# Attention with beacons and a low-rank mixer on one core: first roundings, pair order and the rounding of U and V moved

## The chip, the core and the metric

One core of a Trainium2 chip. Five engines run side by side, each through its own list of instructions in order: TensorE (matrix products and transposes, into PSUM), VectorE, ScalarE, GpSimd (named POOL in the profile) and SyncE (SP). SyncE, ScalarE and GpSimd also issue DMA transfers; only GpSimd's change the number type on the way. PSUM is used as eight tiles in rotation. The metric is the time of one execution on the device, in microseconds (us), lower is better.

## The reference

```python
def _attn_ref(q, k, v, beacon_k, beacon_v):         # 8 batches, 8 heads, 576 tokens, width 64; 16 beacons
    k_all = np.concatenate([beacon_k, k], axis=2)
    v_all = np.concatenate([beacon_v, v], axis=2)
    scores = scale * np.matmul(q, k_all.transpose(0, 1, 3, 2))
    scores = np.where(causal, -1000000000.0, scores)
    a = np.exp(scores - scores.max(-1, keepdims=True))
    a /= a.sum(-1, keepdims=True) + 1e-09
    return np.matmul(a, v_all)

def _moe_ref(x, U, V, w_ch1, w_ch2):                # x: the heads side by side, 576 x 512 per batch
    h = x.transpose(0, 2, 1) @ U @ V                # U: 576 x 32, V: 32 x 576
    u = x + h.transpose(0, 2, 1)
    ch = np.maximum(u @ w_ch1, 0.0) @ w_ch2         # 512 -> 2048 -> 512
    return u + ch
```

All tensors come and go in float32; the kernel computes in 16 bits.

## The kernel before

The work is a row of 32 pairs of heads, four per batch; pair 0 is heads 0 and 1 of batch 0. For a pair, q and k are transposed by TensorE and copied out of PSUM by VectorE (L276), for pair 0 in halves by ScalarE and VectorE. The scores of both heads go into PSUM in two visits of two column groups each (`score_units`, matmuls in L312). Before the products of a visit small matmuls (L304) put the causal mask in, from `identb` and `negmask`. ScalarE turns each group into exponentials (L318), into the tiles `expt`. The values product `av_unit` (L339) multiplies them by `vs`, v with a column of ones, five row blocks one after the other: block j needs the rows of v up to block j. VectorE divides (L347, L348).

When a batch has all eight heads, `mix_units` applies U and V (L368, L404, L416), and `mlp_units` makes units of the channel mixer: sixteen `g_unit` per 512 tokens, four matmuls each (L443), which need `w1`, and then `c_unit` (L459), which need `w2`. Units stand in a queue and are let in between the steps of attention, `FIRST[p]` of them in pair p.

The order on each engine is the order in which the program is written (`tc.manual_schedule`). The start goes so:

- `load_first`: SyncE and ScalarE load q and k of pair 0 and q of pair 1 as float32 (`stq`, `stk`). GpSimd loads the beacon keys.
- `build_masks`: GpSimd makes the identity, issues the load of pair 1's k, and makes the triangular mask; VectorE makes `identb`, `bigmask` and `negmask` from these.
- GpSimd then issues the other half of k and q of batch 0, the beacons of v and the first half of v (L201).
- VectorE fills the gaps of the four `expt` tiles with zeros, and VectorE and ScalarE round first q, then k of pair 0 to 16 bits, each one half (`regroup`, L246, in ScalarE's case L579); k's beacon rows follow (L249).
- `keep_warm` issues matmuls of 128x128 by 128x512 that nobody reads: `IDLE[0]` of them before the first transposes, `IDLE[1]` before pair 0's scores, `IDLE[2]` before pair 1's, `IDLE[3]` before later ones.
- TensorE: pair 0's transposes, its first and second visit, pair 1's transposes (q from `prs[1]`, a rounding by VectorE; k from what GpSimd loaded), pair 1's first visit.
- GpSimd issues the first half of batch 1's k and q, its beacon keys, the second half of v, and the first quarter of `w1` (`emit_w1`).

Then the loop over the eight pairs of batches 0 and 1 begins. Pair p's turn holds the transposes of pair p+2, the second visit of pair p+1, the values products of pair p, and the first visit of pair p+2. In the turn of pair 0, behind the transposes, `load_rest` is called. It begins with `small_loads`: VectorE clears one column of a float32 tile, SyncE loads U in three parts (L151 to L155) and V in four copies (L157) into it, and GpSimd rounds U (L161) and V (L162, L165) to 16 bits. Then GpSimd issues the second half of k and q of batch 1, its beacons and the first half of its v, and the rest of the weights:

```python
def load_rest():
    small_loads()()
    token_load(nc.gpsimd, k[1], kt, HALVES[1])
    token_load(nc.gpsimd, q[1], qt, HALVES[1])
    v_beacon(beacon_v[1], vss[1])
    v_tokens(v[1], vss[1], HALVES[0])
    emit_w1(1)
```

The second half of k and q of batch 1 is first read by the transposes of pair 6 (heads 4 and 5 of batch 1; L260), which open pair 4's turn.

Of the kernel before, what the change touches and what calls it, by code (L numbers as in the profile page):

```python
# [11 lines left out]
F32 = mybir.dt.float32  # L12
# [6 lines left out]
P = 128  # L19
F16_MAX = 65504.0  # L20
# [10 lines left out]
def kernel(  # L31
# [13 lines left out]
    nc = tc.nc  # L45
    B, H, S, D = q.shape
    Nb = beacon_k.shape[2]
# [22 lines left out]
    SLOT = 496  # L70
    EW = 4 * SLOT

    blk = {}
# [14 lines left out]
    gw = [max(o + w for _, _, w, o in g) for g in groups]  # L88
# [13 lines left out]
    def pst(shape, dtype, name):  # L102
        return psum.tile(shape, dtype, tag="ps", name=name)


    ident = const.tile([P, P], F16, name="ident", tag="ident")
    mask = const.tile([P, P], F16, name="mask", tag="mask")
    bigmask = const.tile([P, 4, P], F16, name="bigmask", tag="bigmask")
    identb = const.tile([P, P], BF16, name="identb", tag="identb")
    negmask = const.tile([P, 2, P], BF16, name="negmask", tag="negmask")  # L110

    def build_masks():
        make_identity(nc, ident)
        token_load(nc.gpsimd, k[0], Ls[0][0][0], SETS[1])
        make_upper_triangular(nc, mask, val=F16_MAX, diag=True)
        nc.vector.memset(bigmask[:, 0, P - Nb : P], F16_MAX)
        nc.vector.tensor_copy(out=identb, in_=ident)
        nc.vector.tensor_copy(out=bigmask[:, 0, 0 : P - Nb], in_=mask[:, Nb:P])
        nc.vector.tensor_copy(out=bigmask[:, 1, :], in_=mask)
        for i in range(2):  # L120
            nc.vector.tensor_scalar(
                out=negmask[:, i, :], in0=bigmask[:, i, :], scalar1=1.0, scalar2=NEG,
                op0=ALU.is_lt, op1=ALU.mult,
            )
        for c in range(2, 4):
            nc.vector.tensor_copy(out=bigmask[:, c, :], in_=mask)

    w1 = const.tile([P, NCC, FF], F16, name="w1", tag="w1")
    w2 = const.tile([P, NDC, DM], F16, name="w2", tag="w2")
# [11 lines left out]
    NE = 4  # L141
    expts = [const.tile([P, EW], F16, name=f"expt{i}", tag=f"expt{i}") for i in range(NE)]
# [3 lines left out]
    def small_loads():  # L146

        f = utp.tile([P, NT * R + S], F32, name="small", tag="ut")
        nc.vector.memset(f[:, 0:1], 0.0)
        uf, vf = f[:, 0 : NT * R].rearrange("p (j r) -> p j r", r=R), f[:, NT * R :]  # L150
        nc.sync.dma_start(out=uf[: nq[0], 0, :], in_=moe_U[0 : nq[0], :])  # L151
        nc.sync.dma_start(
            out=uf[:, 1 : NT - 1, :], in_=moe_U[q0[1] : QM, :].rearrange("(j p) r -> p j r", p=P)
        )
        nc.sync.dma_start(out=uf[:NL, NT - 1, :], in_=moe_U[QM:S, :])  # L155
        for cc in range(NCC):
            nc.sync.dma_start(out=vf[ds(R * cc, R), :], in_=moe_V)  # L157

        def cast():
            for rr, jj in ((nq[0], slice(0, 1)), (P, slice(1, NT - 1)), (NL, slice(NT - 1, NT))):  # L160
                nc.gpsimd.tensor_copy(out=Usb[:rr, jj, :], in_=uf[:rr, jj, :])  # L161
            nc.gpsimd.tensor_copy(out=Vsb, in_=vf[:, 0:QM])  # L162
            for cc in range(NCC):
                rs = ds(R * cc, R)
                nc.gpsimd.tensor_copy(out=Vend[rs, cc, :], in_=vf[rs, QM:S])  # L165

        return cast
# [17 lines left out]
    def token_load(eng, src, dst, hs):  # L185
        eng.dma_start(out=dst[0:TP, hs, :], in_=src[hs].rearrange("h (p j) d -> p h (j d)", j=TJ))
# [7 lines left out]
    def v_beacon(bsrc, vs):  # L194
        beacon_load(nc.gpsimd, bsrc, by_head(vs)[:, 0, :, 0:D], ALLH)

    def v_tokens(src, vs, hs, js=range(NT)):
        dst = by_head(vs)[:, :, hs, 0:D]
        for j in js:
            a = Nb if j == 0 else 0  # L200
            nc.gpsimd.dma_start(  # L201
                out=dst[a : a + nq[j], j, :, :], in_=src[hs, ds(q0[j], nq[j]), :].rearrange("h p d -> p h d")
            )
# [24 lines left out]
    def keep_warm(ps, n, a=ident):  # L228


        w = ps.shape[-1] // P
        for _ in range(n):
            nc.tensor.matmul(
                ps[:, 0 : w * P].rearrange("p (a b) -> p a b", b=P), a,
                a.rearrange("p (a b) -> p a b", a=1).broadcast_to([P, w, P]),
                start=True, stop=True,
            )

    def regroup(st, c, i, *copies, beacons=None):

        t = pairs.tile([P, TJ, 2, D], F16, name=f"pr{i}", tag=f"pr{i}")
        src = by_token(st[i][:, 2 * c : 2 * c + 2, :])
        w = TJ // len(copies)
        for a, copy in enumerate(copies):
            js = slice(w * a, w * (a + 1))
            copy(out=t[0:TP, js], in_=src[0:TP, js])  # L246
        if i == 0:
            b = beacons if beacons is not None else src
            copies[0](out=t[TP:TB, TJ - 1], in_=b[TP:TB, TJ - 1])  # L249
        return t  # L250
# [312 lines left out]
    first = []  # L563
# [15 lines left out]
        nc.scalar.activation(out=out, in_=in_, func=AF.Copy)  # L579

    prs = {}

    def regroup_of(p):
        b, c = divmod(p, NH2)
# [16 lines left out]
    def qkT_of(p):  # L601
        b, c = divmod(p, NH2)
        new_qT_of(p)
        copies = [(act_copy, nc.vector.tensor_copy) if p == 0 else (nc.vector.tensor_copy,)] * 2
        turns = by_heads(Ls[b][0], c)
        for i, t in enumerate(prs.get(p, ())):
            if t is not None:
                turns[i] = in_pair(prs[p])[i]
        return qkT_units(turns, qTs[b], kTs[b % 2], c, copies)

    def scores_of(p):
        b, c = divmod(p, NH2)
        return score_units(c, qTs[b], kTs[b % 2], [expts[(2 * p + i) % NE] for i in range(2)], p < NM)
# [19 lines left out]

    QUOTA = {2: 4}

    IDLE = [8, 0, 1, 0]
    queue = []
    state = {"t": 0}

# [38 lines left out]
    with tc.manual_schedule(engines={ENG.PE, ENG.Activation, ENG.DVE, ENG.SP, ENG.Pool}):  # L678
# [3 lines left out]
            token_load(nc.gpsimd, src, dst, HALVES[1])  # L682
        v_beacon(beacon_v[0], vss[0])
        v_tokens(v[0], vss[0], HALVES[0])
        for i in range(NE):

            nc.vector.memset(expts[i][:, SLOT + gw[1] : 2 * SLOT], 0.0)
            nc.vector.memset(expts[i][:, 3 * SLOT + gw[3] : blk[(3, 4)] + P], 0.0)
        V = nc.vector.tensor_copy
        prs[0] = [None, regroup(first, 0, 1, V, act_copy)]  # L690
        prs[0][0] = regroup(first, 0, 0, V, act_copy, beacons=by_token(Ls[0][0][0][:, 0:2, :]))
        keep_warm(pst([P, 512], F32, name="idle"), IDLE[0], plain)
        t0, sc = qkT_of(0), scores_of(0)
        for u in t0:
            u()
        sc[0](IDLE[1])
        sc[1]()
        masks = sc[2]
        prs[1] = [None, regroup(first, 1, 1, V)]
        for u in qkT_of(1):  # L700
            u()
        sc = scores_of(1)
        sc[0](IDLE[2])

# [6 lines left out]
        emit_w1(0)  # L711

        def load_rest():
            small_loads()()
            token_load(nc.gpsimd, k[1], kt, HALVES[1])
            token_load(nc.gpsimd, q[1], qt, HALVES[1])
            v_beacon(beacon_v[1], vss[1])
            v_tokens(v[1], vss[1], HALVES[0])
            emit_w1(1)
            v_tokens(v[1], vss[1], HALVES[1])  # L720
            emit_w1(2)
            emit_w1(3)
            emit_w2()

        NP1 = NF * NH2
        for p in range(NP1):
# [14 lines left out]
            sc = []  # L741
# [170 lines left out]
```

## Time and profile before

| | before |
|---|---|
| median of 3 runs | 360.89 us (360.02 to 362.49) |
| profiled execution | 359.93 us |
| its span, first to last instruction | 358.2 us |
| ScalarE's first run of exponentials starts at | 8.12 us |
| share of the span on the chain that ended last, by TensorE | 86% |

All times inside the execution are counted from the start of the span. The 1.7 us between span and time lie around it. In the rows an engine's name is followed by the line of the kernel, the operation, what is written <- what is read, the sizes, and how many such instructions in a row; the times at the front are start and length, and a bracket gives the idle time before and what ended it. The windows view gives, for each stretch, its length, the busy time of TensorE, of its weight loads, of VectorE, ScalarE and GpSimd with counts, then the mean clock that was granted to TensorE (1.00 is full), the DMA share and GB/s. A row of a DMA ends with the size and the median time from issue to landing.

### The profile page before, as it was taken

Reading aid. Unit: us, or ns where it says so; the run is one execution under the profiler, and the core shown is the slowest. Engines: PE = TensorE matmul, PEld = TensorE weight load, DVE = VectorE, ACT = ScalarE, POOL = GpSimd, SP = SyncE. Lnnn points to the kernel's source line nnn. Section 1 sums busy time; section 2 is a strip of 40 time slices with the busy share of each in tenths; the row PEclk is TensorE's granted clock in tenths of the full one; section 3 lists DMA queues with packets and bytes.
Section 4 is the critical chain, followed back from the end, with each engine's and each line's share of the span. In section 5 each row is a group of like instructions: output and inputs, shape, how many; then the busy total and the mean of one; then the engine's idle time right before and its main releaser. Section 6 shows DMA issues by size and latency. Waiting matters only on the chain.

```text
span 358.2 us, 7821 instructions
## 1 busy us (share of the span) xinstructions
PE 347.8 (97%) x3130; PEld 174.0 (49%) x3130; DVE 187.6 (52%) x485; ACT 166.2 (46%) x356; POOL 97.3 (27%) x139
## 2 busy tenths in 40 slices
PE   6998999999999999999999999999999999999995
PEld 2565455455565444444444444444454444444444
DVE  5585653578986444563456446445645522313311
ACT  4886761469645364367444654456503202401400
POOL 8749611609139028403820400000000000000000
PEclk9898999999999999999999999999999999999999
DMA  8979999999999949995999793142013414013212
GB/s 168 147 111 153 173 208 185 194 173 135 121 76 138 198 103 114 153 198 88 147 143 192 129 135 94 60 100 55 31 60 88 67 59 105 15 59 90 30 51 73
DMA packets 143946, 41.37 MB, mean 115 GB/s; under 512 B 128800, under 2 KB 139296, under 8 KB 143904
## 3 DMA queue, kind: packets, MB, share of 16 engines
q0 software_dynamic: 87408, 18.18, 65.3%
q1 hardware_dynamic: 56272, 22.34, 31.3%
q8 instruction: 26, 0.43, 0.5%
q10 hardware_dynamic: 224, 0.30, 0.3%
q14 instruction: 16, 0.13, 0.1%
HBM read 37.59 MB, written 9.44 MB: 131 GB/s over the span
## 4 chain that ended last, share of the span: by engine, by line
PE 86%; DMA 5%; DVE 3%; SPq 2%; POOL 1%; issue 1%; ACT 0%; POOLq 0%; DVEq 0%
PE gps L443 35%; PE cps L459 32%; PE po L339 7%; PE sps L312 7%; DMA uT<-xb 2%; PE tps L254 2%; DMA small<-in_moe_V_dram 2%; DMA st<-in_q_dram 1%; PE cph L484 1%; SPq L359 1%; DVE kT L276 1%; PE qtp L368 1%; DVE uT L386 1%; DVE qT L276 1%; PE ups L404 1%
## 5 line engine op out<-in xcount | busy, mean ns | idle before, releaser
L318 ACT ACTIVATE expt<-sps 128x496 f16<-128x496 f32 (+2 forms) x256 | 111.4, 534 | 63.9 <-PE sps L312 63.9
L443 PE MATMUL gps<-uT,w 128*128 128x512 f16 x576 | 136.0, 381 | 0.0
L459 PE MATMUL cps<-w,gT 128*128 128x512 f16 x560 | 132.7, 380 | 0.0
L447 ACT ACTIVATE gT<-gps 128x512 f16<-128x512 f32 x86 | 51.9, 608 | 96.3 <-PE gps L443 96.2
L443 PEld LDWEIGHTS <-w 128*128 128x128 f16 x576 | 52.2, 98 | 59.6 <-issue 3.7
L459 PEld LDWEIGHTS <-gT 128*128 128x128 f16 x560 | 49.9, 98 | 59.2 <-issue 6.8
L449 DVE TENSOR_SCALAR gT<-gps 128x512 f16<-128x512 f32 x58 | 40.0, 690 | 48.3 <-PE gps L443 47.2
L472 DVE TENSOR_TENSOR ob<-cps,ut 128x512 f32<-128x512 f32 x31 | 21.4, 690 | 49.6 <-PE cps L459 46.7
L339 PEld LDWEIGHTS <-expt 128*128 128x128 f16 (+1 forms) x960 | 37.0, 98 | 15.7 <-issue 2.5
L201 POOL DMA_DIRECT2D vs<-in_v_dram x50 | 39.6, 807 | 16.3 <-PE po L339 4.2
L339 PE MATMUL po<-vs,expt 128*128 128x65 f16 (+1 forms) x960 | 40.0, 195 | 0.4 <-DVE ob L472 0.2
L312 PE MATMUL sps<-qT,kT 64*128 64x80 f16 (+4 forms) x384 | 35.4, 289 | 1.5 <-DVE kT L281 1.5
L348 DVE TENSOR_TENSOR xb<-po,rec 128x320 f16<-128x320 f32 x64 | 31.5, 492 | 2.2
L289 DVE TENSOR_TENSOR expt<-expt,bigmask 128x512 f16<-128x512 f16 x54 | 22.6, 419 | 11.7 <-ACT expt L318 11.7
L347 DVE RECIPROCAL rec<-po 128x5 f32<-128x5 f32 x64 | 12.0, 187 | 23.5 <-PE po L339 23.5
L312 PEld LDWEIGHTS <-kT 64*128 64x128 f16 x384 | 11.9, 96 | 23.4 <-issue 13.6
L183 POOL DMA_DIRECT2D vs<-in_beacon_v_dram x8 | 4.3, 533 | 61.2 <-PE po L339 61.2
L542 POOL DMA_DIRECT2D st<-in_q_dram x20 | 16.9, 868 | 2.1 <-DMA vs<-in_v_dram 1.8
L542 POOL DMA_DIRECT2D st<-in_k_dram x20 | 16.9, 872 | 1.7 <-DMA vs<-in_v_dram 1.7
L276 DVE COPY qT<-tps 128x576 f16<-128x576 f16 (+1 forms) x16 | 11.8, 737 | 8.7 <-PE tps L254 5.1
L386 DVE TENSOR_TENSOR uT<-ups,uT 128x496 f16<-128x496 f32 x20 | 12.1, 667 | 6.9 <-PE ups L404 3.6
L276 DVE COPY kT<-tps 128x576 f16<-128x576 f16 (+1 forms) x16 | 11.7, 732 | 0.4 <-PE tps L254 0.4
(82 smaller groups left out, 140.3 us busy)
## 6 DMA issues: line engine op xcount, KB each, us to landing
out_dram<-ob SPq DMA_DIRECT2D x35, 256.0 KB, 2.2
vs<-in_v_dram POOLq DMA_DIRECT2D x18, 128.0 KB, 7.8
w<-in_moe_w_ch_dram POOLq DMA_DIRECT2D x4, 512.0 KB, 8.3
w<-in_moe_w_ch_dram POOLq DMA_DIRECT2D x2, 1024.0 KB, 15.3
st<-in_k_dram POOLq DMA_DIRECT2D x12, 128.0 KB, 7.2
st<-in_q_dram POOLq DMA_DIRECT2D x12, 128.0 KB, 9.3
st<-in_k_dram POOLq DMA_DIRECT2D x2, 576.0 KB, 13.6
st<-in_q_dram POOLq DMA_DIRECT2D x2, 576.0 KB, 16.4
```

Source lines behind the costliest of these rows:

```text
L201: nc.gpsimd.dma_start(out=dst[a : a + nq[j], j, :, :], in_=src[hs, ds(q0[j], nq[j]), :].rearrange("h p d -> p h d"))
L276: copy(out=dst[:, c, b0 : b0 + S].rearrange("x (p j) -> x p j", j=TJ)[:, :, js], in_=ps[:, 0:S].rearrange("x (j p) -> x p j", j=TJ)[:, :, js],
L289: nc.vector.tensor_tensor(out=e4, in0=e4, in1=bigmask, op=ALU.min)
L312: nc.tensor.matmul(ps[g, i][:, ds(o, w)], kT[hp, c, ds(P * ch, P)], qT[hp, c, ds(qa, w)], start=not early, stop=True, skip_group_check=early,)
L318: nc.scalar.activation(out=ex[i][:, ds(SLOT * g, gw[g])], in_=ps[g, i][:, 0 : gw[g]], func=AF.Exp, scale=scale)
L339: nc.tensor.matmul(po[:, j, :], ex[0 : nk[c], ds(blk[(c, j)], P)], vs[0 : nk[c], ds(c * H * E + h * E, E)], start=(c == 0), stop=(c == j),)
L348: nc.vector.tensor_tensor(out=xb[:, :, ds(h * D, D)], in0=po[:, :, 0:D], in1=r.broadcast_to([P, NT, D]), op=ALU.mult)
L443: nc.tensor.matmul(g[:, 0:n], w1[:, cc, ts(dc, P)], uT[:, cc, ds(t0, n)], start=(cc == 0), stop=(cc == NCC - 1))
L447: nc.scalar.activation(out=gT["t"][:, dc, 0:n], in_=g[:, 0:n], func=AF.Relu)
L449: nc.vector.tensor_scalar_max(out=gT["t"][:, dc, 0:n], in0=g[:, 0:n], scalar1=0.0)
L459: nc.tensor.matmul(ps[:m, :], gT["t"][:, dc, ds(P * i, m)], w2[:, dc, :], start=(dc == 0), stop=turned and dc == NDC - 1, skip_group_check ...
L542: nc.gpsimd.dma_start(out=dst[a : m[j], j, :, :], in_=src[:, ds(q0[j], nq[j]), :].rearrange("h p d -> p h d"))
```

## The change

Three things are moved.

1. In `build_masks`, VectorE's first column fill of `bigmask` and `identb` go ahead of the load of pair 1's k, and the rounding of pair 0's q goes ahead of the copies that make `bigmask` and `negmask`. The last two copies into `bigmask` and the zero fills of `expt` go into a function `clear`, called behind pair 1's transposes.
2. Pair 1's transposes go ahead of pair 0's second visit, k before q, and two warm matmuls (`IDLE[4]`) ahead of them. `IDLE[1]` becomes 2, so two more stand before pair 0's scores.
3. In `load_rest`, `small_loads` is called first and still issues its loads there, but its roundings on GpSimd are issued behind the second half of k and q of batch 1 and its v beacons.

```diff
     def build_masks():
         make_identity(nc, ident)
+        nc.vector.memset(bigmask[:, 0, P - Nb : P], F16_MAX)
+        nc.vector.tensor_copy(out=identb, in_=ident)
         token_load(nc.gpsimd, k[0], Ls[0][0][0], SETS[1])
         make_upper_triangular(nc, mask, val=F16_MAX, diag=True)
-        nc.vector.memset(bigmask[:, 0, P - Nb : P], F16_MAX)
-        nc.vector.tensor_copy(out=identb, in_=ident)
+        prs[0] = [None, regroup(first, 0, 1, V, act_copy)]
...
+
+    def clear():
         for c in range(2, 4):
             nc.vector.tensor_copy(out=bigmask[:, c, :], in_=mask)
+        for i in range(NE):
+            nc.vector.memset(expts[i][:, SLOT + gw[1] : 2 * SLOT], 0.0)
+            nc.vector.memset(expts[i][:, 3 * SLOT + gw[3] : blk[(3, 4)] + P], 0.0)
...
-    IDLE = [8, 0, 1, 0]
+    IDLE = [8, 2, 1, 0, 2]
...
-        for i in range(NE):
-
-            nc.vector.memset(expts[i][:, SLOT + gw[1] : 2 * SLOT], 0.0)
-            nc.vector.memset(expts[i][:, 3 * SLOT + gw[3] : blk[(3, 4)] + P], 0.0)
-        V = nc.vector.tensor_copy
-        prs[0] = [None, regroup(first, 0, 1, V, act_copy)]
         prs[0][0] = regroup(first, 0, 0, V, act_copy, beacons=by_token(Ls[0][0][0][:, 0:2, :]))
...
         sc[0](IDLE[1])
-        sc[1]()
         masks = sc[2]
         prs[1] = [None, regroup(first, 1, 1, V)]
-        for u in qkT_of(1):
+        keep_warm(pst([P, 512], F32, name="idle"), IDLE[4])
+        for u in qkT_of(1)[::-1]:
             u()
+        clear()
+        sc[1]()
         sc = scores_of(1)
         sc[0](IDLE[2])
...
         def load_rest():
-            small_loads()()
+            cast_small = small_loads()
             token_load(nc.gpsimd, k[1], kt, HALVES[1])
             token_load(nc.gpsimd, q[1], qt, HALVES[1])
             v_beacon(beacon_v[1], vss[1])
+            cast_small()
             v_tokens(v[1], vss[1], HALVES[0])
             emit_w1(1)
```

More of the change, by code (lines that the diff above doesn't have):

```diff
@@ L581 @@
     prs = {}
+    V = nc.vector.tensor_copy
     def regroup_of(p):
```

## The prediction, made before the changed kernel was run

> **What bounds the kernel now.** I read the page's busy times first, then the waits of TensorE over the first 100 us, then the chain of waits over the first 60 us.
>
> ```profile
> PE 347.8 (97%) x3130; PEld 174.0 (49%) x3130; DVE 187.6 (52%) x485; ACT 166.2 (46%) x356; POOL 97.3 (27%) x139
> ```
>
> ```profile
> 190.00:270.00 80.00, 80.00 (x722) 38.74 (x719) 41.69 (x110) 39.62 (x87) 4.71 (x6) 1.00 0.57 92
> ```
>
> ```profile
> PE tps L260 <- DMA st<-in_q_dram: 1.8, 1, 1.8
> ```
>
> TensorE is busy for 97% of the span, and in the window from 190 to 270 us it never stops. So microseconds can be had only near the start, and a shift that TensorE has gained there should last to the end. Near the start the longest wait is one of 1.8 us for a query load. The chain says how that load came to be late:
>
> ```profile
> 18.08 5.50 DMA small<-in_moe_V_dram
> 23.73 0.60 POOL Vsb L162
> 25.44 0.62 POOL st L186
> 26.06 5.07 DMA st<-in_q_dram
> 31.17 1.00 PE tps L260 x24
> ...
> 33.81 1.43 PE gps L443 x4
> 35.70 0.87 PE gps L443 x4
> ```
>
> GpSimd's queue stands at the rounding of V (L162) until V lands at 18.08 + 5.50 = 23.58. Only behind the roundings does it issue batch 1's second key half (25.44) and second query half (26.06), and the transposes of pair 6 (L260) get them at 31.17. The rows also give two paces of the same four mixer matmuls, 1.43 and 0.87. The windows view says why; I cut it at 3.41 us, since with cuts there the granted clock (the column behind POOL's) comes out as one value per window:
>
> ```profile
> 4.11:7.52 3.41, 1.49 (x19) 0.80 (x18) 2.98 (x20) 1.71 (x4) 3.41 (x6) 1.00 1.08 181
> 7.52:10.93 3.41, 3.41 (x36) 1.90 (x36) 1.17 (x2) 2.81 (x7) 2.43 (x4) 0.50 1.60 163
> 10.93:14.35 3.42, 2.98 (x56) 1.77 (x53) 2.37 (x5) 2.45 (x7) 2.13 (x4) 1.00 1.54 132
> 24.59:28.00 3.41, 2.85 (x64) 2.05 (x58) 2.13 (x6) 1.70 (x6) 3.29 (x8) 1.00 0.33 34
> 28.00:31.41 3.41, 1.66 (x30) 0.79 (x30) 1.65 (x3) 3.22 (x8) 3.41 (x5) 1.00 1.60 186
> 31.41:34.83 3.42, 3.42 (x48) 2.17 (x43) 2.99 (x8) 1.53 (x4) 3.42 (x6) 0.50 1.47 137
> ```
>
> A window in which TensorE was busy for 1.49 or 1.66 us is followed by one at clock 0.50; windows with 2.85 and 2.98 us are not. So the query wait costs twice: 1.75 us of standing, and then half speed from 31.41 to 34.83.
>
> The Trainium skill ("TensorE: Matmul & The Clock Gate", Part 1, the HAM clock gate) also has a free-running window of about 3.4 us, and under "HAM oscillation" it gives the rule "no PE-idle gaps >~3.4µs". By that rule a 1.75 us gap would not have cooled the engine; here it did, and the trace decides.
>
> **The first parts: q rounded first, pair 1's transposes first.** VectorE's rounding of q (L246) moves ahead of the mask copies and fills:
>
> ```profile
> 3.81 0.52 ACT L579 ACTIVATE pr<-stq 96x384 f16<-96x384 f32 x1 [0.51 <-DMA stq<-in_q_dram]
> 4.87 0.52 ACT L579 ACTIVATE pr<-stk 96x384 f16<-96x384 f32 x1 [0.54 <-DMA stk<-in_k_dram]
> ```
>
> ```profile
> 4.80 0.52 DVE L246 CAST pr<-stq 96x384 f16<-96x384 f32 x1
> 5.25 0.53 DVE L246 CAST pr<-stk 96x384 f16<-96x384 f32 x1
> ```
>
> ScalarE shows when the data is there: q at 3.81, k at 4.87. VectorE can round q at 3.81 instead of 4.80, and then k at 4.87 instead of 5.25: 0.4 us sooner for the first scores, since these need k too. Queued behind the new wait for q are the mask copies, whose reader (L304) comes after the transposes. The fills and two copies go behind pair 1's transposes, where nobody reads them before the first values product. Four more 128x512 warm matmuls cost 0.87 (warm) to 1.43 us (cold) of TensorE. Pair 1's transposes ahead of pair 0's second score visit delay that visit by their own length, and let pair 1 follow at once.
>
> What of this reaches the end? Look at TensorE's first values product (L339), the v loads that it needs, as GpSimd issues them and with their time to landing, and ScalarE's exponentials (L318):
>
> ```profile
> 14.11 0.69 PE L339 MATMUL po<-vs,expt 128*128 128x65 f16 x9
> 14.95 0.85 PE L339 MATMUL po<-vs,expt 128*128 128x65 f16 x21
> ```
>
> ```profile
> 7.13 2.13 POOL L201 DMA_DIRECT2D vs<-in_v_dram  x3
> ```
>
> ```profile
> vs<-in_v_dram POOLq DMA_DIRECT2D x2, 64.0 KB, 7.2
> ```
>
> ```profile
> 16.42 8.65 ACT L318 ACTIVATE expt<-sps 128x496 f16<-128x496 f32 x20 [0.56 <-PE sps L312]
> ```
>
> The product stops after nine matmuls, exactly where it first needs row block 3 of v. That load is the second of the three from 7.13, so issued at 7.13 + 0.71 = 7.84 (2.13 over three is 0.71), and takes 7.2: it lands at 15.0. No edit moves it. Whatever the front gains ahead of 14.95 is waited away there, and ScalarE's run from 16.42 starts when it did. I take 0 for all of these parts. If that cover were gone, their worth would lie between +1.4 (the warm matmuls, cold) and -1.0 (the q rounding's whole 4.80 - 3.81).
>
> **The moved roundings.** GpSimd will issue key half, query half and v beacon before it rounds. Does its queue let it?
>
> ```profile
> 4.49 0.67 POOL L186 DMA_DIRECT2D st<-in_q_dram  x1
> ```
>
> ```profile
> 12.12 0.67 POOL L186 DMA_DIRECT2D st<-in_q_dram  x1 [2.04 <-DMA st<-in_q_dram]
> ...
> 16.97 0.77 POOL L172 DMA_DIRECT2D w<-in_moe_w_ch_dram  x1
> ...
> 27.25 3.59 POOL L201 DMA_DIRECT2D vs<-in_v_dram  x5
> ```
>
> ```profile
> st<-in_q_dram POOLq DMA_DIRECT2D x1, 288.0 KB, 5.9
> ```
>
> ```profile
> vs<-in_v_dram POOLq DMA_DIRECT2D x1, 40.0 KB, 3.3
> ```
>
> The issue at 12.12 waited for the query load of 4.49, eight issues earlier, so I assume eight in flight. The key half would then wait for the load of 12.12 to land, 12.12 + 5.9 = 18.0, against 16.97 + 0.77 = 17.74 when the queue is free. With some 0.67 for each of three it is through at 20.0, ahead of V's landing, so V's rounding still starts at 23.73, the roundings end at 25.4 as before, and their readers see no change. The three issues hide in a wait, and everything behind them (five v loads, w1, w2) goes out 27.25 - 25.4 = 1.85 us sooner. SyncE's own loads keep their order. The query half, issued at 18.7, has over 10 us until 29.4 where it took 5.07. If V landed later, every microsecond would come off the 1.85.
>
> **What is late next.** Pair 6's transposes can follow pair 5's scores:
>
> ```profile
> 28.73 0.69 PE L312 MATMUL sps<-qT,kT 64*128 64x496 f16 x4
> 29.38 1.97 ACT L318 ACTIVATE expt<-sps 128x496 f16<-128x496 f32 x4
> ```
>
> They start at 29.42 instead of 31.17: 1.75. With the clock kept, the next 3.4 us are not at half speed: up to another 1.7, so 3.45 at most. Two things cut that. The first mixer matmul needs a PSUM tile that, counting the rotation of eight, the fourth of ScalarE's exponentials from 29.38 frees, at 31.35. And batch 1's fifth v load, issued near 28.3, lands near 28.3 + 3.3 = 31.6, which the product ahead of that matmul needs. So the matmul starts at about 31.65, not 33.81, a gain of 2.16, and runs in 0.87, not 1.43: 2.16 + 0.56 = **2.7 us**, carried to the end. On the profiled execution's 359.93 this gives 357.2. That execution lies 0.96 below the median of the runs (360.89), so I forecast 360.89 - 2.7 = **358.2**.
>
> A second cover, further on, is batch 2's load:
>
> ```profile
> 62.92 0.94 DVE L246 COPY pr<-st 96x768 f16<-96x768 f16 x2
> ```
>
> ```profile
> 64.54 0.42 PE L254 MATMUL tps<-ident,pr 96*128 96x96 f16 x6
> ```
>
> The query is regrouped at 62.92 + 0.47 = 63.4 and used at 64.54, a margin of 1.1. TensorE coming 2.7 sooner needs the loads at least 1.6 sooner; they are issued 1.85 sooner.
>
> **Rivals.** *The front cools the clock.* With a warm front TensorE gets back up to half of the window from 7.52, 1.7 us, and then stands twice: for pair 2's query half, issued at 4.49, and for v until 15.0.
>
> ```profile
> st<-in_q_dram POOLq DMA_DIRECT2D x1, 288.0 KB, 7.3
> ```
>
> That half lands at 11.8. If the two waits take 1.1 us off the 2.98 busy from 10.93 to 14.35, 1.9 are left, near the 1.66 that cooled it. Half speed from 14.95 to 17.76, the end of the next window, then loses 1.4. Little of it comes back, as ScalarE's run from 16.42 goes on for 8.65 us without a pause. Of 2.7 about 1.3 is left: 359.6. Against: the windows may lie elsewhere in other runs, and the threshold may be anywhere between 1.66 and 2.85.
>
> *Only the wait goes.* If the half clock at 31.41 had another cause than the gap, it stays, and the gain is 1.75: 359.1. The two low windows, each followed by 0.50, speak against it. The rule of the Trainium skill quoted above ("TensorE: Matmul & The Clock Gate") speaks for it.
>
> *The loads set the pace.* If batch 2's query lands no sooner, because the DMA engines are full from 28 us on, TensorE waits at 64.54 and keeps 1.1: 359.8. The DMA engines' 34 GB/s in 24.59 to 28.00 speaks against: there is room, and the halves fill it.
>
> *Slower: V is held back.* If V's rows were moved behind the two halves, 2 x 288 KB at 186 GB/s add 3.2 us: V at 26.8, roundings done at 28.6, the last of five v issues near 31.5, landing at 34.8, so the first mixer matmul at 34.8 instead of 33.81, 1.0 later. TensorE idles before it, so a half-speed window follows that costs up to 1.7, where before had (34.83 - 33.81) / 2 = 0.5 left of one: 1.2 more. Together 2.2: 363.1. It decides once V is more than about 2 us late.
>
> ```profile
> w<-in_moe_w_ch_dram POOLq DMA_DIRECT2D x4, 512.0 KB, 8.3
> ```
>
> Against: the w1 load of 16.97 needs 8.3, so it lands near 25.3, and V, issued after it on the other queue, landed at 23.58: V overtakes GpSimd's transfers. The Trainium skill says the same ("DMA: Bandwidth & Descriptors", Queues, rings and completion order): each DMA engine takes turns among its queues, packet by packet.
>
> *More than forecast.* PSUM and v are no limits, or other runs of before held more half-speed windows than the profiled one (360.02 to 362.49): 3.5 or more, 357.4 and below.
>
> **How the numbers follow.** The forecast has 0.41, the cooled front 0.26, only the wait 0.08, the loads 0.08, V held back 0.10, more 0.07. The range from 356.8 to 360.6 holds all but V and the far end of the last, some 0.83 less the spread of a median of a few runs. About 1% (3.6 us) is what a measurement of this kernel can tell from no change. Faster by that needs less than 357.3: "more", and a third of the forecast's spread, 0.20. Slower by it needs over 364.5, the worst of V held back: 0.06. The rest, 0.74, is within 1%.
>
> **What would show it.** In the profile after: the key and query halves issued near 18 to 19; no wait of L260 for the query near 30; clock 1.00 through 31 to 35; the first mixer matmul near 31.7; ScalarE's long run starting at 16.4 in spite of first scores some 0.4 sooner; v's third block still ending the wait at 15.0. A clock of 0.50 between 14 and 18 shows the first rival; V landing past 25.6 the slower one; a wait at the second regrouping near 61 the loads.

## The result and the profile after

| | before | changed |
|---|---|---|
| median of 8 runs each | 361.84 us (360.02 to 362.58) | 358.31 us (356.14 to 359.05) |
| ratio, with 95% interval | | 0.9893 (0.9859 to 0.9926) |
| profiled execution | 359.93 us | 358.65 us |
| its span | 358.2 us | 357.0 us |
| its mean granted clock | 0.990 | 0.995 |

The medians are 3.5 us apart where 2.7 were forecast; the ratio says 1.07% faster, just outside the 1% band around no change, and its interval reaches back into the band, where the prediction had put 0.74 of its chance. That the median lies 0.1 us from the forecast 358.2 is partly luck: the median of before stands 0.95 us above the 360.89 that the forecast started from, and the gain is 0.8 us larger. (The ratios are estimated separately, with their intervals; they are not the quotients of the two medians, and can differ from these by some tenths of a per cent.) The profiled execution of the changed kernel is one of its longer ones, so the two profiles differ by only 1.2 us. Line numbers of the changed kernel are six higher than before in the code below the masks: the values product is L345, the mixer matmul L449, the transposes L266, the exponentials L324.

GpSimd's part of the timeline (start, length, work, and in brackets the idle time before with what ended it) answers to the rows of L162 and L186 in the prediction:

```profile
18.47 0.68 POOL L192 DMA_DIRECT2D st<-in_k_dram  x1 [1.55 <-DMA st<-in_q_dram]
19.14 0.68 POOL L192 DMA_DIRECT2D st<-in_q_dram  x1
...
24.61 0.60 POOL L168 CAST Vsb<-small 128x496 f16<-128x496 f32 x1 [3.43 <-PE sps L318]
25.16 1.17 POOL L171 CAST Vend<-small 32x80 f16<-32x80 f32 x4
26.28 3.59 POOL L207 DMA_DIRECT2D vs<-in_v_dram  x5
```

The key and query halves go out at 18.47 and 19.14, ahead of the rounding of V, and the issues wait for a query load as the eight in flight of the prediction demand. But V is rounded at 24.61 and not 23.73, so the five v loads of batch 1 are 27.25 - 26.28 = 0.97 us earlier, not 1.85. (The name in the bracket at 24.61 is not the releaser: V's last copy, issued at 17.58, took 6.9 us to land, until 24.5.)

TensorE's timeline shows what became of the three waits of the prediction:

```profile
13.52 1.24 PE L345 MATMUL po<-vs,expt 128*128 128x65 f16 x30
...
20.37 0.45 PE L345 MATMUL po<-vs,expt 128*128 128x65 f16 x9
21.23 0.31 PE L345 MATMUL po<-vs,expt 128*128 128x65 f16 x5 [0.42 <-DMA vs<-in_v_dram]
22.53 1.03 PE L345 MATMUL po<-vs,expt 80*128 80x65 f16 x16 [0.98 <-DMA vs<-in_v_dram]
...
30.97 0.71 PE L266 MATMUL tps<-ident,st 96*64 96x96 f16 x24
33.02 1.03 PE L449 MATMUL gps<-uT,w 128*128 128x512 f16 x4
```

The first values product runs from 13.52 through all its thirty matmuls: the wait for v that ended at 14.95 is gone. Pair 6's transposes at 30.97 wait for nothing: the query wait of 1.75 is gone. In their place stand 0.42 and 0.98 us at pair 2's values product, which needs the second half of batch 0's v. The windows around it, cut at 3.41 us (length, busy times of TensorE, weight loads, VectorE, ScalarE and GpSimd, then the granted clock), show that TensorE, busy for 2.10 us in the window of this standing, runs at half speed in the next:

```profile
19.03:22.44 3.41, 2.10 (x50) 1.41 (x43) 1.50 (x4) 3.08 (x8) 1.94 (x6) 1.00 1.34 209
22.44:25.85 3.41, 3.32 (x44) 2.34 (x44) 1.37 (x4) 1.27 (x3) 1.12 (x4) 0.50 1.15 176
```

So this execution keeps full speed where before had lost it (31.41 to 34.83) and loses it nine us sooner. The first mixer matmul comes at 33.02, 0.79 ahead of the 33.81 of before, and takes 0.87 instead of 1.43: 1.35 us, of which 1.2 are seen in the span.

The runs of the changed kernel fall into two groups. A half-speed window of 3.41 us takes 0.5 x 3.41 / 357 = 0.0048 off a run's mean clock, so the clock counts them: of fourteen runs (eight here, six of the same kernel beside later experiments) nine have a clock of 0.998 or more and a median of 356.42 us, five have 0.994 or 0.995, one such window, and a median of 358.66. One run of the first group took 358.37 at clock 1.0; why is open. The 70 runs of before that stand beside the experiments have 0.979 to 0.995, on average 2.2 such windows.

### The profile page after: what moved, and what is told of

It reads as the page before. It is cut to its first block, busy times and chain, and to the rows that moved or that the text cites. A ratio compares the mean times of both kernels' runs of the same rounds, so it can differ in the third digit from the quotient of the medians.

```text
span 357.0 us, 7830 instructions
## 1 busy us (share of the span) xinstructions
PE 348.2 (98%) x3134; PEld 174.1 (49%) x3134; DVE 188.1 (53%) x485; ACT 166.1 (47%) x356; POOL 97.4 (27%) x139
## 4 chain that ended last, share of the span: by engine, by line
PE 90%; DMA 4%; POOL 2%; DVE 2%; ACT 1%; issue 1%; POOLq 0%
PE gps L449 36%; PE cps L465 34%; PE po L345 8%; PE sps L318 7%; DMA vs<-in_v_dram 2%; DMA st<-in_q_dram 2%; PE tps L260 1%; PE cph L490 1%; PE qtp L374 1%; POOL vs L207 1%; PE ups L385 1%; PE ups L410 1%; POOL st L192 1%; DVE uT L392 1%; ACT expt L324 0%
## 5 line engine op out<-in xcount | busy, mean ns | idle before, releaser
L324 ACT ACTIVATE expt<-sps 128x496 f16<-128x496 f32 (+2 forms) x256 | 111.3, 533 | 63.6 <-PE sps L318 63.5
L449 PE MATMUL gps<-uT,w 128*128 128x512 f16 x576 | 135.4, 379 | 0.0
L449 PEld LDWEIGHTS <-w 128*128 128x128 f16 x576 | 52.0, 98 | 59.3 <-issue 3.2
L345 PEld LDWEIGHTS <-expt 128*128 128x128 f16 (+1 forms) x960 | 37.6, 99 | 17.5 <-issue 3.8
L345 PE MATMUL po<-vs,expt 128*128 128x65 f16 (+1 forms) x960 | 40.5, 195 | 1.8 <-DMA vs<-in_v_dram 1.4
## 6 DMA issues: line engine op xcount, KB each, us to landing
st<-in_k_dram POOLq DMA_DIRECT2D x2, 576.0 KB, 13.1
```

What stands on the lines that cost most here:

```text
L324: nc.scalar.activation(out=ex[i][:, ds(SLOT * g, gw[g])], in_=ps[g, i][:, 0 : gw[g]], func=AF.Exp, scale=scale)
L345: nc.tensor.matmul(po[:, j, :], ex[0 : nk[c], ds(blk[(c, j)], P)], vs[0 : nk[c], ds(c * H * E + h * E, E)], start=(c == 0), stop=(c == j),)
L449: nc.tensor.matmul(g[:, 0:n], w1[:, cc, ts(dc, P)], uT[:, cc, ds(t0, n)], start=(cc == 0), stop=(cc == NCC - 1))
```

## The experiments

The theory: the moved roundings bring the gain, by the loads and a small part by the clock, and the front gains about 1 us that a later wait takes back. The rivals: the front brings the gain; the clock brings it; the loads of U and V, or the warm matmuls, matter more than the order of the roundings. All ratios are to runs of the kernel before on the same chip.

### Each half alone

**Roundings only**: the kernel before, with part 3 of the change.

```diff
-            small_loads()()
+            cast_small = small_loads()
             token_load(nc.gpsimd, k[1], kt, HALVES[1])
             token_load(nc.gpsimd, q[1], qt, HALVES[1])
             v_beacon(beacon_v[1], vss[1])
+            cast_small()
```

> Only part 3 of the change: the roundings of U and V behind the three issues; the front as before. Theory of the prediction (all of the gain comes from here): some 2.7 us less than before, a ratio near 0.9925, with no wait of pair 6's transposes for the query and clock 1.00 behind 31 us. Rival (the front brings most of it): less than 1.3 us, a ratio of 0.996 or above.

**Front only**: the changed kernel with `small_loads()()` back in its old place (the same diff in reverse).

> Only parts 1 and 2: q rounded first, pair 1's transposes first, four more warm matmuls; the roundings of U and V as before. Theory of the prediction (the first values product waits for v's third block, and takes back what the front gains): ratio 1.000, within 0.002. Rival (v lands sooner too, as in the profile after, where the loop began 1.0 us sooner): 1.0 us or more is kept, a ratio of 0.997 or below. Second rival (the loop only runs sooner into the second half of batch 0's v and cools there): slower, 1.003 or above.

| | median | before beside it | ratio |
|---|---|---|---|
| roundings only (9 runs) | 358.86 us | 362.11 us | 0.9922 (0.9895 to 0.9949) |
| front only (12 runs) | 361.25 us | 362.11 us | 0.9982 (0.9956 to 1.0007) |

By the ratios the roundings alone give 0.0078 x 362.1 = 2.8 us (1.8 to 3.8; the medians are 3.3 apart); the front alone gives 0.6 (0.9 by the medians), not clear of zero. TensorE's timeline with the roundings only:

```profile
29.64 0.71 PE L260 MATMUL tps<-ident,st 96*64 96x96 f16 x24
...
31.23 0.62 PE L339 MATMUL po<-vs,expt 128*128 128x65 f16 x15 [0.23 <-ACT expt L318]
31.69 1.03 PE L443 MATMUL gps<-uT,w 128*128 128x512 f16 x4
```

The transposes come at 29.64 and the first mixer matmul at 31.69 (forecast 29.42 and 31.65), and the 0.23 us that TensorE still stands is ended by ScalarE, the limit that the prediction named. The window from 31.41 to 34.82 has clock 1.00:

```profile
4.80:8.21 3.41, 1.77 (x24) 1.09 (x25) 2.97 (x10) 1.77 (x4) 3.41 (x6) 1.00 1.17 175
8.21:11.62 3.41, 3.39 (x39) 2.02 (x38) 1.57 (x4) 3.10 (x8) 1.81 (x4) 0.51 1.83 154
11.62:15.04 3.42, 3.42 (x45) 1.97 (x42) 1.50 (x4) 2.18 (x5) 3.42 (x6) 0.50 1.25 137
...
31.41:34.82 3.41, 3.41 (x44) 1.75 (x41) 3.28 (x10) 2.39 (x7) 3.41 (x5) 1.00 1.35 169
```

This execution has two half-speed windows in its front and yet a span of 355.3 us, 1.7 less than that of the changed kernel with one window later on. So the number of half-speed windows alone does not set the time; that it matters where they fall is likely, but the two kernels differ in their front too.

With the front only, TensorE waits for v and for the query:

```profile
21.46 0.31 PE L345 MATMUL po<-vs,expt 128*128 128x65 f16 x5 [0.62 <-DMA vs<-in_v_dram]
22.44 1.04 PE L345 MATMUL po<-vs,expt 80*128 80x65 f16 x16 [0.67 <-DMA vs<-in_v_dram]
...
32.17 0.71 PE L266 MATMUL tps<-ident,st 96*64 96x96 f16 x24 [1.25 <-DMA st<-in_q_dram]
```

The query wait of 1.25 us stays, and the new wait at pair 2 is there without part 3: it belongs to the front.

### The clock by itself

The kernel before, with eight warm matmuls where it stands for the query; nothing is moved.

```diff
             b, c = divmod(p, NH2)
+            if p == NH2:
+                keep_warm(pst([P, 512], F32, name="idle"), 8)
```

> The kernel before with eight warm matmuls of 128x512 ahead of pair 6's transposes, where TensorE stands for 1.75 us waiting for the query; nothing else is moved, the wait stays. If the half clock behind it comes from that standing, it goes: up to 1.65 us less, a ratio near 0.9955, clock 1.00 from 31 to 35. If only the wait itself costs, or the gap does not cool the engine: ratio 1.000.

Measured: 361.18 us (12 runs) to 362.11, ratio 0.9985 (0.9958 to 1.0012): 0.5 us, not clear of zero, and far below the 2.8 of the roundings. Its profiled execution has clock 1.0 throughout:

```profile
28.36 1.90 PE L233 MATMUL idle<-ident 128*128 128x512 f16 x8
31.00 0.71 PE L260 MATMUL tps<-ident,st 96*64 96x96 f16 x24 [0.73 <-DMA st<-in_q_dram]
...
33.07 0.39 PE L339 MATMUL po<-vs,expt 128*128 128x65 f16 x6 [0.36 <-DMA vs<-in_v_dram]
33.30 1.03 PE L443 MATMUL gps<-uT,w 128*128 128x512 f16 x4
```

The matmuls fill the wait, but the query comes no sooner, and behind it batch 1's v ends a wait at 33.07. A warm TensorE reaches the first mixer matmul only 0.5 us ahead of before, and its matmuls take 0.87 us instead of 1.43. So the earlier loads bring most of the gain; the clock's part is of the size of the forecast's 0.56, but the twelve runs allow anything from a gain of 1.5 us to a loss of 0.4. Over the 70 runs of before, time rises by 0.41 us for each half-speed window (least squares, 95% interval 0.20 to 0.62; 0.31 when each chip is compared with itself), which is no proof of cause.

### The warm matmuls and the wait at pair 2

**No new warm matmuls**: the changed kernel with the four added ones taken out.

```diff
-    IDLE = [8, 2, 1, 0, 2]
+    IDLE = [8, 0, 1, 0, 0]
```

> The changed kernel with IDLE[1] and IDLE[4] at 0, that is without its four added warm matmuls. If the front is waited away at v's third block: as the changed kernel, a ratio to before near 0.989. If the warm matmuls keep the clock up through the first scores and this reaches the end: about 1 us more than the changed kernel, a ratio of 0.992, and clock 0.50 somewhere from 7 to 11 us.

Measured: 356.78 us (6 runs, 356.04 to 360.49), ratio 0.9896 (0.9851 to 0.9942); the changed kernel has 0.9893. The four matmuls do nothing that shows in the time, though four of these six runs have a clock of 0.988 to 0.995, and five of the fourteen runs of the changed kernel are that low. TensorE's waits (us in total, times, longest) and its timeline in this profile, of span 354.5 us:

```profile
PE po L345 <- DMA vs<-in_v_dram: 1.5, 2, 1.2
```

```profile
31.14 1.03 PE L449 MATMUL gps<-uT,w 128*128 128x512 f16 x4
```

The wait at pair 2 is as long as in the changed kernel's profile (1.4), but no window is cooled, and the first mixer matmul comes at 31.14, 1.88 ahead of 33.02. A half-speed window with 3.32 us of work in it costs half of that, 1.66. So it is the cooled window more than the wait that makes these two profiles differ, as far as two executions can say.

**Eight, then four, warm matmuls in the wait** at pair 2 of the changed kernel:

```diff
-            seq += [prior] + av_of(p)
+            seq += [prior]
+            if p == 2:
+                seq.append(lambda: keep_warm(pst([P, 512], F32, name="idle"), 8))
+            seq += av_of(p)
```

> The changed kernel with eight warm matmuls of 128x512 (1.73 us at full clock) ahead of pair 2's values products, where the profile after stands for 0.42 and 0.98 us waiting for the second half of batch 0's v. If the half clock from 22.4 to 26.0 in that profile comes from this standing, it goes and the wait itself stays: up to 1.7 us less than the changed kernel in the runs that cool there, ratio to before near 0.985, and a narrower spread. If the standing is not what cools it, or the cooling is hidden by ScalarE: as the changed kernel or up to 0.3 us slower, 0.989 to 0.990.

> As the run with eight warm matmuls ahead of pair 2's values products, with four of them (0.87 us at full clock). If a standing that is cut short is enough to keep the clock, and eight were more than the wait had room for: all runs in the group of 356 to 357, ratio to before 0.985 or below, clock 0.998 or above in all runs. If four are too few: some runs near 358.5 with a clock of 0.995, as the changed kernel; ratio 0.987 to 0.989.

Measured: with eight 357.60 us (6 runs, 356.31 to 357.80), ratio 0.9877 (0.9852 to 0.9903), every clock 0.998 or more; with four 357.52 us (4 runs, 357.23 to 358.33), ratio 0.9854 (0.9837 to 0.9871). With eight, no run is near 358.7, and only one is below 357. That looks as if the fill cost a little in every run and the cooled window more in some, but it is not shown: of the six runs of the changed kernel beside these only one was long, and their median is 0.8 us lower (356.77, below). Neither fill is faster than the changed kernel beyond the intervals. With four, one run of the four has a clock of 0.994. It is the profiled one, and its half-speed window lies ahead of the fill, so it does not say whether four are enough; it shows the rival of the cooled front at its own place:

```profile
10.79:14.20 3.41, 2.07 (x49) 1.53 (x48) 1.50 (x4) 3.25 (x9) 2.43 (x4) 1.00 1.48 144
14.20:17.61 3.41, 3.29 (x47) 2.31 (x48) 1.37 (x4) 1.24 (x5) 3.08 (x5) 0.52 1.47 137
```

### The loads of U and V

**U and V one pair later**: their loads move from 13.8 to 17.3 us, and the roundings and batch 1's first v loads with them.

```diff
         def load_rest():
-            cast_small = small_loads()
             token_load(nc.gpsimd, k[1], kt, HALVES[1])
             token_load(nc.gpsimd, q[1], qt, HALVES[1])
             v_beacon(beacon_v[1], vss[1])
-            cast_small()
+
+        def load_later():
+            small_loads()()
...
+                if p == 1 and i == 1:
+                    load_later()
```

> The changed kernel with SyncE's loads of U and V issued one pair later (behind pair 3's transposes, near 17 us instead of 13.8); GpSimd's order stays. If these loads are what makes the second half of batch 0's v land at 22.5 instead of 20 to 21, it lands by 21 and pair 2's values products wait less than 0.3 us; the roundings of U and V then end near 27.5 instead of 26.3, so batch 1's v gives a part back: ratio 0.985 to 0.990. If they are not, the wait at 20.8 to 22.5 stays and the later roundings only cost: ratio 0.991 or above.

**The same, with batch 1's first v loads issued between the roundings of U and of V** (`small_loads` now returns the two roundings as two functions):

```diff
-            small_loads()()
+            cast_u, cast_v = small_loads()
+            cast_u()
             v_tokens(v[1], vss[1], HALVES[0])
+            cast_v()
```

> As the run with the later loads of U and V, and batch 1's first half of v is issued between the rounding of U and that of V. If the roundings hold batch 1's v back, the first mixer matmul comes near 31 us and the ratio is 0.983 or below. If V's rounding, now behind five more issues, is late for its reader instead, TensorE waits there near 28 us: as the run without the split or slower.

Measured: 361.60 us (12 runs) to 361.75, ratio 1.0000 (0.9977 to 1.0023), and 360.56 us (12 runs), ratio 0.9977 (0.9949 to 1.0004). The whole gain is gone in the first, most of it in the second. Two rows for one load, the last block of batch 0's v, issued near 15.5 in both kernels (size, us from issue to landing): first the changed kernel, then U and V later.

```profile
vs<-in_v_dram POOLq DMA_DIRECT2D x1, 40.0 KB, 7.0
```

```profile
vs<-in_v_dram POOLq DMA_DIRECT2D x1, 40.0 KB, 4.0
```

With U and V out of the way v lands 3.0 us sooner, and TensorE's timeline has pair 2's product in one piece. What that costs stands further on:

```profile
20.19 1.09 PE L345 MATMUL po<-vs,expt 128*128 128x65 f16 x30
...
32.14 0.30 PE L345 MATMUL po<-vs,expt 128*128 128x65 f16 x3 [0.85 <-DMA vs<-in_v_dram]
...
34.00 0.49 PE L345 MATMUL po<-vs,expt 128*128 128x65 f16 x6 [0.95 <-DMA vs<-in_v_dram]
34.30 1.90 PE L449 MATMUL gps<-uT,w 128*128 128x512 f16 x4
```

GpSimd's timeline has the cause:

```profile
26.69 0.60 POOL L168 CAST Vsb<-small 128x496 f16<-128x496 f32 x1 [1.68 <-DMA small<-in_moe_V_dram]
27.23 1.17 POOL L171 CAST Vend<-small 32x80 f16<-32x80 f32 x4
28.35 3.58 POOL L207 DMA_DIRECT2D vs<-in_v_dram  x5
```

This is the slower rival forced into being, since V's loads now start behind the two halves: V rounded at 26.69 (the rival had it landing at 26.8), batch 1's v issued 1.1 us later than before, a mixer that starts at 34.30 and at half speed (1.90 for four matmuls). In the second kernel batch 1's v ends no wait any more, but the step that applies V waits for V itself, in the list of TensorE's waits:

```profile
PE ups L412 <- POOL Vsb L170: 2.0, 1, 2.0
```

**The changed kernel again, and its roundings split**: the first is the changed kernel as it is, run beside the two kernels above; the second has the split of the last diff, with U's and V's loads where the changed kernel has them.

> The changed kernel once more, beside the others. All theories: ratio near 0.989, runs in two groups near 356.2 and 358.5. If the second group comes from a half-speed window behind the wait for the second half of batch 0's v, its runs have a mean clock of 0.995 and the first group's 0.998 or above.

> The changed kernel with batch 1's first half of v issued between the rounding of U and that of V; the loads of U and V stay where they are. In the profiles of the changed kernel the first mixer matmul stood for batch 1's v in one of two. If that is a common loss, v comes some 3 us sooner and the ratio is 0.001 to 0.003 below the changed kernel's, 0.984 or below. If V's rounding, now some 3.6 us of issues later, is late for its reader: TensorE waits there, near 28 to 29 us, and the ratio is 0.990 or above.

Measured: again, 356.77 us (6 runs, 356.19 to 359.36), ratio 0.9854 (0.9827 to 0.9880); split, 357.14 us (8 runs) to 360.90, ratio 0.9897 (0.9863 to 0.9931). The first gives 5.0 us by the medians, more than the 3.5 of its first eight runs: one of these six runs is of the longer group, and four of those eight by their clock.

Its long run, 359.36 us at clock 0.995, is the profiled one. The expectation placed its half-speed window behind pair 2's product. It is not there: pair 2 waits 0.42 us and keeps the clock, and TensorE stands further on, for batch 1's v. GpSimd's row of V's rounding and TensorE's rows:

```profile
25.04 0.60 POOL L168 CAST Vsb<-small 128x496 f16<-128x496 f32 x1 [3.39 <-DMA small<-in_moe_V_dram]
```

```profile
31.60 0.28 PE L345 MATMUL po<-vs,expt 128*128 128x65 f16 x4 [0.59 <-DMA vs<-in_v_dram]
32.10 0.31 PE L345 MATMUL po<-vs,expt 128*128 128x65 f16 x5 [0.22 <-DMA vs<-in_v_dram]
32.71 0.19 PE L345 MATMUL po<-vs,expt 80*128 80x65 f16 x1 [0.30 <-DMA vs<-in_v_dram]
32.74 1.15 PE L449 MATMUL gps<-uT,w 128*128 128x512 f16 x4
```

V comes 1.3 us later than the 23.73 of before, so the five v loads go out at 26.70, only 0.55 us sooner, and the half-speed window follows at 33.50. Pair 6's transposes wait for no query here either (29.11). The two profiles of the changed kernel, both of its longer group, are thus cooled at two different places.

The split does not help: in its GpSimd queue the fifth v load has to wait for the first weights, and goes out at 25.25 when in the changed kernel it can go at about 29.

```profile
25.25 0.65 POOL L209 DMA_DIRECT2D vs<-in_v_dram  x1 [1.54 <-DMA w<-in_moe_w_ch_dram]
```

Its first mixer matmul comes at 31.13, the 31.14 of the run without warm matmuls: v four us sooner moves nothing there, since ScalarE's exponentials end the wait ahead of it in both (0.23 us).

### The parts of the front

The changed kernel with pair 0's second visit back ahead of pair 1's transposes and no new warm matmuls (roundings and early q):

```diff
-    IDLE = [8, 2, 1, 0, 2]
+    IDLE = [8, 0, 1, 0]
...
+        sc[1]()
         masks = sc[2]
         prs[1] = [None, regroup(first, 1, 1, V)]
-        keep_warm(pst([P, 512], F32, name="idle"), IDLE[4])
-        for u in qkT_of(1)[::-1]:
+        for u in qkT_of(1):
             u()
         clear()
-        sc[1]()
```

> The moved roundings of U and V with the first part alone: q rounded ahead of masks and fills, pair 1's transposes behind the second visit as before, no added warm matmuls. If the front's share of the gain comes from the first part: as the changed kernel, ratio 0.985 to 0.989, and no half-speed window near 7 to 11 us. If it comes from the order of pair 1: as the moved roundings alone, 0.992, and a half-speed window there.

The changed kernel with masks, fills and the first roundings in the old order (roundings, new pair order, warm matmuls):

```diff
-        nc.vector.memset(bigmask[:, 0, P - Nb : P], F16_MAX)
-        nc.vector.tensor_copy(out=identb, in_=ident)
...
+        nc.vector.memset(bigmask[:, 0, P - Nb : P], F16_MAX)
+        nc.vector.tensor_copy(out=identb, in_=ident)
-        prs[0] = [None, regroup(first, 0, 1, V, act_copy)]
...
+        clear()
+        prs[0] = [None, regroup(first, 0, 1, V, act_copy)]
...
-        clear()
```

> The moved roundings with the second part alone: pair 1's transposes ahead of the second visit, with the four warm matmuls; q is rounded behind masks and fills as before. If the front's share comes from the order of pair 1, or from its warm matmuls: ratio 0.985 to 0.989 and no half-speed window near 7 to 11 us. If it comes from the first part: 0.992.

Measured, to 360.90: 357.01 us (7 runs), ratio 0.9896 (0.9860 to 0.9933), and 357.49 us (6 runs), ratio 0.9908 (0.9877 to 0.9939). The first is about as fast as the changed kernel's first eight runs, and yet its profiled execution (span 356.0 us) has two half-speed windows in its front, so neither of its two expectations holds as a whole:

```profile
8.00:11.41 3.41, 3.40 (x38) 1.95 (x37) 1.80 (x11) 3.04 (x8) 2.04 (x3) 0.51 1.75 166
11.41:14.83 3.42, 3.42 (x47) 2.08 (x44) 1.62 (x9) 2.29 (x5) 3.19 (x5) 0.50 1.34 140
```

Roundings only had 0.9922 (0.9895 to 0.9949), the changed kernel 0.9893 and 0.9854. The first interval of the changed kernel overlaps that of the roundings only; the second (0.9827 to 0.9880, on another chip) does not. So the front probably adds something to the roundings, by the ratios 0.3% to 0.7%, but how much, and which of its parts does it, stays open. In the profiles with both parts of the front in which no window up to there is cooled, the first mixer matmul comes at 31.00 (eight warm matmuls), 31.13 (split) and 31.14 (no new warm matmuls), 0.5 to 0.7 us ahead of the 31.69 with the roundings only; with the new order alone it comes at 31.70, no sooner.

No kernel tried is faster than the changed one by more than the intervals.

## Why the prediction was right, and where it was not

**The moved roundings** were right in mechanism and size. Eight in flight, key half near 18, queries without a wait, ScalarE as the next limit, the mixer at 31.65: the run with this part alone shows each (17.86, 29.64, 0.23 us, 31.69) and gives 2.8 us for 2.7. That the sizes agree so closely is partly luck: the forecast took its 31.65 from batch 1's v, landing at 31.6, and there v's last block landed at about 31.3 (28.5 + 2.8) and ScalarE ended the wait; and the gain is known to 1 us only. In the changed kernel's own profile the mixer starts at 33.02, behind the half-speed window from 22.44, which costs up to 1.7 us.

**"The roundings end at 25.4 as before"** was mis-sized: V was ready at 24.61 and 25.04 in the changed kernel's two profiles, at 23.97 with the roundings only and at 22.85 without the warm matmuls. With the old order of the roundings it was ready between 22.97 and 23.73 in three profiles. The scatter is as large as the difference, so these runs cannot tell whether the two halves hold V back a little. The microseconds come off the 1.85, as the prediction said they would: 0.97 and 0.55 are left.

**"No edit moves it"** is the step that failed: that v's third block lands at 15.0 and takes back whatever the front gains. That time was one execution's. The load took 7.2 us there and about 6.1 in the changed kernel's profile (7.84 + 6.1 = 13.9), and by the same sum the block landed between 13.1 and 14.3 in the profiles of the experiments with the kernel's old front or its new one. So the loop does begin sooner: pair 3's transposes start at 15.41 instead of 16.45, and ScalarE's exponentials go in one unbroken run from 10.45 where 16.42 was forecast:

```profile
10.45 11.66 ACT L324 ACTIVATE expt<-sps 128x496 f16<-128x496 f32 x28 [0.15 <-PE sps L318]
```

The early q is not what does it here: in this execution q was there at 4.23 and not at 3.81, and the first exponentials start at 8.34, later than the 8.12 of before (7.79 in the kernel's second profile and with the front only, near the forecast 0.4 us sooner). In this profile and in that of the front only, the gain is then waited away at the second half of v (pair 2), and with the front only once more at the query of pair 6. That the front alone is worth about 0 came out nearly right (0.6 us, not clear of zero), but by luck, through other waits than the one named; behind the moved roundings it may be worth more. A load that hides an edit hides it only by its margin, and that margin was known from one execution.

**The clock** term, 0.56, agrees with the 0.5 us of the warm matmuls in before's query wait, but that size is not clear of zero. *Only the wait goes* falls: the window at 31.41 has clock 1.00 in the run with the roundings only. That a wait of 1.75 us cooled TensorE, against the rule of the Trainium skill ("TensorE: Matmul & The Clock Gate", HAM oscillation) that only gaps over about 3.4 us matter, the runs confirm with shorter ones: 0.42 and 0.98 us of standing in one window, followed by half speed.

**The cooled front** was put at 14.95 to 17.76 and priced at 1.4 us. It stood there in one profile (four warm matmuls at pair 2), at pair 2's product in the changed kernel's first profile, and behind batch 1's v in its second. One half-speed window somewhere goes with the step from 356.4 to 358.7 us; that the front places it is not shown. **V held back** was right as a mechanism: forced, with V's loads behind the halves, it took the whole gain. In the changed kernel V's loads start ahead of GpSimd's two halves (15.14 against 18.47), and V was at most 1.3 us late, short of the 2 us at which this rival was to decide. **The loads set the pace** is out. The 63.35 of batch 2's transposes in the changed kernel's first profile, 1.19 ahead of 64.54, cannot show it, as the rival allowed 1.1. With the roundings only they come at 62.02, 2.5 ahead and without a wait, behind a query regrouped at 61.1 instead of 63.4.

**The size**: the total of 3.5 us is over the 2.7, and the later six runs give 5.0 (their median, 356.77, is at the lower end of the range). This is what was called *more than forecast*. Part of it may be that before has 2.2 half-speed windows per run, and the changed kernel 0.4 (five in fourteen runs): 1.8 windows at 0.41 us are 0.7, of which the sum held 0.56 for one. How much of the rest is the front, and how much the scatter of the medians, can't be told.

## What to carry to other kernels

A rounding that waits for a slow load holds everything behind it on a queue that also issues DMAs; move the issues ahead of it as far as the queue's transfers in flight allow, and check that they do not delay the load it waits for. When a wait hides an edit, name the next load behind that wait as well, and take landing times from more than one execution before counting on them. Where the mean clock of a run tells how many windows ran at half speed, use it: it says what happened in runs that have no profile.

## What the hardware showed

**Waits of little over 1 us halve the clock in some executions and not in others.** In the aligned windows at full clock, TensorE busy for 2.01 us of 3.41 or less was always followed by half speed, and 2.58 or more never; in between both occur. (A window that is itself at half speed is another matter: with the roundings only, one with 3.39 us of work is followed by a second.) Two windows of one execution, the changed kernel run again, have almost the same busy time:

```profile
9.61:13.02 3.41, 2.08 (x41) 1.08 (x37) 1.28 (x14) 3.26 (x9) 0.96 (x2) 1.00 1.57 108
13.02:16.43 3.41, 3.41 (x86) 2.51 (x79) 2.88 (x9) 2.46 (x7) 3.41 (x6) 1.00 1.07 141
...
30.09:33.50 3.41, 2.07 (x25) 1.13 (x20) 2.57 (x8) 2.44 (x7) 3.41 (x6) 1.00 1.19 107
33.50:36.91 3.41, 3.41 (x25) 1.41 (x22) 1.53 (x4) 0.45 (x1) 3.40 (x5) 0.50 1.80 173
```

The first holds a wait of 1.23 us for pair 2's query and is not followed by half speed; the second holds the waits for batch 1's v and is. So busy time alone does not decide between them. Nor does the number of matmuls, 41 and 25: the windows above with 50 and 49 matmuls (2.10 and 2.07 us busy) were followed by half speed too. What is counted stays open. Where the windows start differs between executions: aligned to their half-speed windows, those of before's profile have a cut at 4.11 us, those of the changed kernel's two profiles at 5.37 and 6.19. So the same wait can fall into one window or across two.

**SyncE's loads of U and V slow GpSimd's v loads.** The last 40 KB block of batch 0's v took 4.0 us in the two kernels that load U and V later, and 4.5 to 7.0 us in the twelve profiles in which they are loaded beside it. The prediction used the sharing of the DMA engines only in V's favour (V overtakes the weights); here it works the other way, and it lengthens the wait that the front runs into at pair 2.
